# An LSH attention and expert kernel on one core: joint value means, sign words and sums on GpSimd, a new order of the work

## The chip, the cores and the metric

The kernel runs on one core of a Trainium2 chip. The core has a matrix engine (TensorE, "PE" in the rows; its weight loads are "PEld"), a vector engine (VectorE, "DVE"), a scalar engine (ScalarE, "ACT"), a general engine (GpSimd, "POOL"), and a queue engine (SyncE, "SP") that here only issues transfers. Each engine takes its own instructions strictly in the order in which they stand. The metric is the device time of one execution in microseconds (us); the number to forecast is a median over repeated runs. Three runs of the kernel before took 1003.26, 1003.40 and 1003.53 us.

## The reference

Inputs are q, k, v of 4 batches x 8 heads x 768 positions x 64, a 64x6 projection, and the two matrices of a feed-forward layer.

```
q_bucket = sum over 6 bits of 2^bit * (q @ proj > 0)          # k_bucket likewise
mask     = q_bucket[:, None] == k_bucket[None, :]
scores   = where(mask, q @ k.T / 8, -1e9)
attn     = exp(scores - max);  attn /= sum(attn) + 1e-9
x        = attn @ v, heads side by side                       # 3072 x 512
out      = (s * relu(x @ w_in)^2 + b) @ w_out                 # 512 -> 2048 -> 512
```

## The kernel before

**Staging.** There are 32 visits, one for each batch and head, and each has three chunks of 256 queries: 96 slots. A slot computes scores in three PSUM banks (L595 or L597), takes their maximum on VectorE (L603), turns it with small TensorE transposes (L614, L618), adds a row with mask and maximum (L635 or L637), takes exponentials on ScalarE (L642), and multiplies by the values (L665, or L667 and L668) into PSUM bank 3. ScalarE empties that bank (L698, L700); two heads are normalised together on VectorE and GpSimd (L707 to L712) and written to DRAM as `xd`. The first nine visits (`NPL = 9`: batch 0 and one head of batch 1) multiply in whole fp32, where one product shows as two records in the trace; later visits split each operand into a high and a low part and use a faster format.

**The feed-forward layer.** `moe` (L746 and L763) runs chunk by chunk as soon as the eight heads of a batch are done (`GATE = 23`). Its products carry the lowest priority, so TensorE takes them wherever attention leaves room. The weights come as raw 64-bit words and are rebuilt in `decode`, 32 tiles of 128x512: ScalarE makes a shifted value and the scaled low word (L374, L375), VectorE takes the sign bit (L376) and joins it to the shifted word (L377), GpSimd adds the low word (L378), ScalarE rounds to the high part (L380) and GpSimd subtracts it (L386). Two tiles `osb` take turns. All decoding lies in the first 210 us, beside batch 0.

**The mean of the values.** Because of the 1e-9 in the denominator each head adds a constant times the sum of its values (`vmn`, a bias of L700). `prep_values` makes that sum two visits ahead. In the first nine visits TensorE adds six 128x64 value tiles with six one-column products (`sums`, L543). In the 23 later ones VectorE adds the six tiles (L556) and TensorE makes one one-column product (L558). Both write PSUM bank 4, which the small transposes of the scores use as well; the values of later visits arrive in one tile, `vn`.

**The order.** A planner (`Plan`) collects all steps with a cost, inputs, outputs and a priority, and lays them out with a model of five engines. To a step's priority it adds a number from the table `NUDGE`, by the step's place in the source and the part of the program. What comes out is a fixed instruction order for each engine.

Of the kernel before, what the change touches and what calls it, by code (L numbers as in the profile page):

```python
# [15 lines left out]
ALU = mybir.AluOpType  # L16
# [156 lines left out]
def lsh_attention_moe(ctx: ExitStack, tc, q, k, v, proj, w_in, w_out, s, b, out):  # L173
# [43 lines left out]
    def dve(n, fn, r, w, pr, ns=None):  # L217
        plan.add(DVE, ((n + 64) / 960.0 if ns is None else ns), fn, r, w, pr)
# [7 lines left out]
    def mmc(n, c):  # L226
        return c * (n / 2400.0 + 0.0013) if c % 4 == 0 else c * (n * 0.000436 + 0.0088)
# [124 lines left out]
    def decode(u, pr):  # L352
# [23 lines left out]
        dve(256, lambda: nc.vector.tensor_scalar(raw()[:, :, 1], gi, -2**31, None, ALU.bitwise_and), [gk], rk, pr, 0.6)  # L376
        dve(512, lambda: nc.vector.scalar_tensor_tensor(gi, gi, 3, raw()[:, :, 1], ALU.logical_shift_left, ALU.bitwise_or), rk, [gk], pr, 0.92)  # L377
# [8 lines left out]
        pool(512, lambda: nc.gpsimd.tensor_tensor(wt[key][:, 1], g, f32(wt[key][:, 0]), ALU.subtract), [gk, key + (0,)], [key + (1,)], pr)  # L386
# [135 lines left out]
    def mean(bb, h, pr):  # L522

        n = bb % 2 * H + h
        act(1, lambda: nc.scalar.activation(vmn[:, n:n + 1], bank[0:D, 4, 0:1], AF.Copy, scale=EPS / (S + EPS)), [("b", 4, "m")], [("vm", n)], pr)
        plan.hold(None)

    def prep_values(w, pr):
        bb, h = visits[w]["bb"], visits[w]["h"]
        x = visits[w]["x"]  # L530
        vk = [("vs", x, 0), ("vs", x, 1)]
        vd = v[bb, h].rearrange("(p t) d -> p t d", t=NT)
        if w < NPL:
            if x not in SETS:
                def new():
                    EV[x] = wk.tile([P, NT, 2, D], F32, tag=f"vs{x}", name=f"vs{w}")
                plan.add(None, 0.0, new, [], vk, pr)
                pool(1, lambda: nc.gpsimd.memset(EV[x][:, :, 1], 1.0), [], vk[1:2], pr, 0.5)
            plan.add(SP, 0.7, lambda: nc.sync.dma_start(EV[x][:, :, 0], vd), [], vk[0:1], pr, 0.9)

            def sums():
                for t in range(NT):
                    nc.tensor.matmul(bank[0:D, 4, 0:1], EV[x][:, t, 0], ones, start=(t == 0), stop=(t == NT - 1))  # L543
            plan.hold(4)
            pe(0.5, sums, vk, [("b", 4, "m")], pr)
            mean(bb, h, pr)
            return

        def new():
            VS[x] = wk.tile([P, NT, 2, D], F32R, tag=f"vs{x}", name=f"vs{w}")  # L550
        plan.add(None, 0.0, new, [], vk, pr)
        to = vn
        plan.add(SP, 0.7, lambda: nc.sync.dma_start(to, vd), [], ["vn"], pr, 0.9)
        act(NT * D, lambda: nc.scalar.copy(VS[x][:, :, 0, :], to), ["vn"], vk[0:1], pr)
        pool(NT * D, lambda: nc.gpsimd.tensor_tensor(VS[x][:, :, 1, :], to, f32(VS[x][:, :, 0, :]), ALU.subtract), ["vn", vk[0]], vk[1:2], pr)
        dve(NT * D, lambda: nc.vector.tensor_reduce(pj[:, 0:D], to.rearrange("p t d -> p d t"), AX.X, ALU.add), ["vn"], ["vp"], pr, 0.84)  # L556
        plan.hold(4)
        pe(0.25, lambda: nc.tensor.matmul(bank[0:D, 4, 0:1], pj[:, 0:D], ones, start=True, stop=True), ["vp"], [("b", 4, "m")], pr)  # L558
        mean(bb, h, pr)
# [397 lines left out]
```

## Time and profile before

| what | value |
|---|---|
| median of three runs | 1003.4 us |
| the profiled execution's own time | 1000.88 us |
| its span, first to last instruction | 999.1 us |
| TensorE busy | 979.9 us, 98% |
| VectorE, ScalarE, GpSimd busy | 677.5, 670.8, 640.5 us |
| mean granted TensorE clock | 0.998 of full speed |

The span is what the trace shows; 1.8 us of the profiled execution lie around it. The profiled execution was 2.5 us shorter than the median run. Busy time of TensorE counts a matmul from start to its modelled end, and matmuls overlap, so the distance from one start to the next tells more than a duration.

### The profile page before, as it was taken

What the parts mean: (1) busy time and instruction counts of PE and PEld (TensorE: products, weight loads), DVE (VectorE), ACT (ScalarE), POOL (GpSimd) and SP (SyncE); (2) the same over time, 40 slices, a digit from 0 to 9 for tenths busy, and PEclk for the clock granted to TensorE, in tenths of its full rate; (3) what the DMA queues carried; (4) which work ended last, traced back from release to release, by engine and by line L of the source; (5) the groups of instructions that cost most, each with busy time, mean ns of one, the idle gap of its engine ahead of it and who ended that gap; (6) DMA issues with size and microseconds to landing.
All of it is one profiled execution on the core that took longest, in us unless ns stands there. A gap on an engine that the chain in (4) does not pass through costs nothing.

```text
span 999.1 us, 18150 instructions
## 1 busy us (share of the span) xinstructions
PE 979.9 (98%) x6528; PEld 883.6 (88%) x6528; DVE 677.5 (68%) x1030; ACT 670.8 (67%) x1312; POOL 640.5 (64%) x584
## 2 busy tenths in 40 slices
PE   8989989999999999999999999999999999999998
PEld 6877868889999999999999999999999999999997
DVE  6777888778778877878778877878778766200000
ACT  4677777767767777777767777777777777523232
POOL 1677776758677677768677677778677677522222
PEclk9999999999999999999999999999999999999999
DMA  7575664533423423433423432433423310201000
GB/s 195 148 192 162 182 169 129 152 76 82 129 53 79 122 69 63 131 71 81 120 63 79 104 84 61 136 71 81 120 60 80 97 47 1 96 1 64 32 22 21
DMA packets 131954, 93.06 MB, mean 93 GB/s; under 512 B 101145, under 2 KB 104601, under 8 KB 131865
## 3 DMA queue, kind: packets, MB, share of 16 engines
q1 hardware_dynamic: 126664, 74.87, 29.9%
q10 hardware_dynamic: 5200, 17.05, 5.7%
q8 instruction: 51, 0.84, 0.3%
q14 instruction: 39, 0.31, 0.1%
HBM read 48.24 MB, written 18.87 MB: 67 GB/s over the span
## 4 chain that ended last, share of the span: by engine, by line
PE 91%; DVE 2%; POOL 2%; DMA 2%; issue 1%; ACT 1%; DVEq 0%; ACTq 0%; SPq 0%; POOLq 0%
PE bank L746 28%; PE bank L763 27%; PE bank L597 6%; PE bank L637 6%; PE bank L667 5%; PE bank L668 5%; PE bank L665 4%; PE bank L595 2%; PE bank L695 2%; DMA xd<-xsb 1%; PE bank L618 1%; PE bank L506 1%; PE bank L508 1%; PE bank L507 1%; POOL w L386 1%
## 5 line engine op out<-in xcount | busy, mean ns | idle before, releaser
L661 POOL TENSOR_TENSOR hl<-et,hl 128x512 fp32r<-128x512 f32 x207 | 267.3, 1320 | 138.5 <-ACT hl L660 86.0
L746 PE MATMUL bank<-xc,w 128*128 128x256 f32 x2304 | 338.5, 284 | 0.0
L746 PEld LDWEIGHTS bank<-xc,w 128*128 128x128 f32 x2304 | 305.4, 190 | 5.9
L763 PE MATMUL bank<-w,ghb 128*128 128x512 f32 x768 | 252.4, 396 | 0.0
L754 POOL TENSOR_TENSOR glb<-rb,ghb 128x512 fp32r<-128x512 f32 x96 | 124.1, 1292 | 99.8 <-ACT ghb L753 93.7
L603 DVE TENSOR_REDUCE mx<-bank 128x256 f32<-128x1536 f32 x96 | 168.0, 1750 | 6.9 <-PE bank L597 3.2
L763 PE MATMUL bank<-w,glb 128*128 128x512 f32 x384 | 152.3, 398 | 0.0
L642 ACT ACTIVATE et<-bank 128x512 f32<-128x512 f32 x234 | 128.6, 626 | 32.5 <-PE bank L637 23.4
L763 PEld LDWEIGHTS bank<-w,ghb 128*128 128x128 f32 x768 | 135.2, 189 | 16.6 <-issue 0.2
L687 DVE TENSOR_REDUCE zb<-et 128x256 f32<-128x1536 f32 x69 | 120.8, 1751 | 40.9 <-ACT et L642 40.2
L660 ACT CAST hl<-et 128x512 fp32r<-128x512 f32 x207 | 125.2, 672 | 0.3
L751 ACT ACTIVATE rb<-bank 128x512 f32<-128x512 f32 x96 | 56.8, 592 | 98.7 <-PE bank L746 98.4
L597 PE MATMUL bank<-aq,ks 84*128 84x256 f32 x504 | 109.6, 301 | 2.3 <-DMA aq<-nat 1.4
L700 ACT ACTIVATE xpb<-bank,vmn 64x256 f32<-64x256 f32 x96 | 45.0, 468 | 97.4 <-PE bank L668 64.1
L667 PE MATMUL bank<-hl,vs 128*128 128x256 f32 x414 | 107.9, 283 | 0.0
L668 PE MATMUL bank<-hl,vs 128*128 128x256 f32 x414 | 107.3, 281 | 0.0
L597 PEld LDWEIGHTS bank<-aq,ks 84*128 84x128 f32 x504 | 81.0, 190 | 9.1 <-ACT xpb L700 1.8
L667 PEld LDWEIGHTS bank<-hl,vs 128*128 128x128 f32 x414 | 77.9, 188 | 8.9
L668 PEld LDWEIGHTS bank<-hl,vs 128*128 128x128 f32 x414 | 78.0, 188 | 8.0
L763 PEld LDWEIGHTS bank<-w,glb 128*128 128x128 f32 x384 | 72.2, 188 | 11.5 <-issue 0.2
L637 PE MATMUL bank<-bq,ks 128*128 128x256 f32 x504 | 76.9, 287 | 0.0
L771 DVE SCALAR_TENSOR_TENSOR osb<-bank,misc,bcs 128x512 f32<-128x512 f32 x22 | 16.2, 747 | 88.9 <-PE bank L763 88.8
(126 smaller groups left out, 1545.2 us busy)
## 6 DMA issues: line engine op xcount, KB each, us to landing
xd<-xsb SPq DMA_DIRECT2D x48, 256.0 KB
xc<-xd SPq DMA_DIRECT2D x48, 256.0 KB
raw<-in_moe_w_in_dram ACTq DMA_DIRECT2D x16, 512.0 KB
raw<-in_moe_w_out_dram ACTq DMA_DIRECT2D x16, 512.0 KB
out_dram<-osb SPq DMA_DIRECT2D x22, 256.0 KB
ks<-aq SPq DMA_DIRECT2D x28, 192.0 KB
ks<-bq SPq DMA_DIRECT2D x28, 192.0 KB
bq<-aq SPq DMA_DIRECT2D x28, 192.0 KB
```

Source lines behind the costliest of these rows:

```text
L597: nc.tensor.matmul(o, ks[0:HR + NR, 0, kt], aq[0:HR + NR, cs], start=m == 0, stop=m == 1, skip_group_check=True)
L603: dve(S * TPC, lambda: nc.vector.tensor_reduce(t, sc, AX.XY, ALU.max), [("b", b) for b in pb], [tk], pr, 1.75)
L637: nc.tensor.matmul(o, ks[:, 1, kt], bq[:, cs], start=False, stop=m == 1, skip_group_check=True)
L642: act(512, lambda p=p, z=z: nc.scalar.activation(et(z) if plain(i) else pairs(z), bank[:, pb[p]] if plain(i) else bank[:, pb[p]].rearrange ...
L660: act(512, lambda z=z, y=y: nc.scalar.copy(HL[2 * y].rearrange("p (m n) -> p m n", n=CH), pairs(z)), [("e", z)], [("hl", 2 * y)], pr, 0.05)
L661: pool(512, lambda z=z, y=y: nc.gpsimd.tensor_tensor(HL[2 * y + 1].rearrange("p (m n) -> p m n", n=CH), pairs(z), f32(HL[2 * y]).rearrange ...
L667: nc.tensor.matmul(av, VS[x][:, kt], HL[2 * y][:, ms], start=(kt == 0), stop=False)
L668: nc.tensor.matmul(av, VS[x][:, kt], HL[2 * y + 1][:, ms], start=False, stop=(kt == NT - 1))
L687: dve(S * TPC, lambda: nc.vector.tensor_reduce(ZB, es, AX.XY, ALU.add), [("e", z) for z in range(NE)], ["zb"], pr, 1.75)
L746: nc.tensor.matmul(hp, wt[("wi", n, cc)][:, m % 2, fs], xc[:, m // 2, :], start=(cc == 0 and m == 0), stop=(cc == NC_ - 1 and m == 2))
L754: pool(2 * CH, lambda r=r, gh=gh, gl=gl: nc.gpsimd.tensor_tensor(gl, r, f32(gh), ALU.subtract), [rk, hk], [lk], MP)
L763: nc.tensor.matmul(bank[:, 6 + t, :], (gh, gh, gl)[n][:, ts], wt[("wo", f)][:, n % 2], start=(f == 0 and n == 0), stop=(f == NF - 1 and n ...
```

## The change

Three things are edited. For odd and even heads of one batch the two value sums stand side by side in `pj`, and one product with 128 columns of weights instead of 64 gives both means; for it the odd head's values are loaded into `vn` one more time. For visits 2 to 8 GpSimd adds the six value tiles in three instructions (128x192, 128x64, 128x64), and TensorE makes one product instead of six. In `decode` the sign word is made by GpSimd with a comparison and a multiplication. The planner's costs are adjusted, and the table `NUDGE` has new numbers throughout (80 rows before, 84 after).

```
-        return c * (n / 2400.0 + 0.0013) if c % 4 == 0 else c * (n * 0.000436 + 0.0088)
+        return c * (n / 2400.0 + 0.0013) if c % 4 == 0 else c * {256: 0.1215, 384: 0.175, 512: 0.2345}[n]
...
-        dve(256, lambda: nc.vector.tensor_scalar(raw()[:, :, 1], gi, -2**31, None, ALU.bitwise_and), [gk], rk, pr, 0.6)
-        dve(512, lambda: nc.vector.scalar_tensor_tensor(gi, gi, 3, raw()[:, :, 1], ...), rk, [gk], pr, 0.92)
+        pool(512, lambda: nc.gpsimd.tensor_scalar(raw()[:, :, 1], g, 0.0, -2.0**31, ALU.is_lt, ALU.mult), [gk], rk, pr, 0.65)
+        dve(512, lambda: nc.vector.scalar_tensor_tensor(gi, gi, 3, raw()[:, :, 1], ...), rk, [gk], pr, 0.8)
...
+            if w > 1:
+                s1, s2 = vn[:, 0:3], vn[:, 3]
+                pool(3 * D, lambda: nc.gpsimd.tensor_tensor(s1, EV[x][:, 0:3, 0], EV[x][:, 3:6, 0], ALU.add), vk[0:1], ["vn"], pr, 0.56)
+                pool(D, lambda: nc.gpsimd.tensor_tensor(s2, vn[:, 0], vn[:, 1], ALU.add), [], ["vn"], pr, 0.27)
+                pool(D, lambda: nc.gpsimd.tensor_tensor(s2, vn[:, 3], vn[:, 2], ALU.add), [], ["vn"], pr, 0.27)
+                plan.hold(4)
+                pe(0.3, lambda: nc.tensor.matmul(bank[0:D, 4, 0:1], s2, ones, start=True, stop=True), ["vn"], [("b", 4, "m")], pr)
+                mean(bb, h, pr)
...
+        if h % 2 and w > NPL:
+            return
+        heads = (h,) if h % 2 else (h, h + 1)
+        for j, h_ in enumerate(heads):
+            if j:
+                fetch(to, tk, v[bb, h_].rearrange("(p t) d -> p t d", t=NT))
+            sums(j, to, tk)
+        rows = len(heads) * D
         plan.hold(4)
-        pe(0.25, lambda: nc.tensor.matmul(bank[0:D, 4, 0:1], pj[:, 0:D], ones, start=True, stop=True), ["vp"], [("b", 4, "m")], pr)
-        mean(bb, h, pr)
+        pe(0.3, lambda: nc.tensor.matmul(bank[0:rows, 4, 0:1], pj[:, 0:rows], ones, start=True, stop=True), ["vp"], [("b", 4, "m")], pr)
+        for j, h_ in enumerate(heads):
+            mean(bb, h_, pr, j)
...
-    0: {0: -25.2, 1: 58.1, 2: 23.3, 3: 60, 4: -47.5},
+    0: {0: -6.4, 1: -4.1, 2: -23.8, 3: -11.2, 4: 11},
```

Line numbers move: in the changed kernel the sign word is still L376 and the join L377, but scores' transposes are L640 and L644 (were L614, L618), the row that is added is L651 on VectorE (was L625) and L661 or L663 on TensorE (were L635, L637), attention times values in fp32 is L691 (was L665), the means are L546, L553 and L582 (were L543 and L558).

In the first decodes, GpSimd's order before, with the add L378 and the subtraction L386 (`raw` and `w` with their buffer numbers):

```order
L378 TENSOR_TENSOR osb<-osb,raw_209 128x512
L386 TENSOR_TENSOR w_365<-osb,w_365 128x512
L386 TENSOR_TENSOR w_377<-osb,w_377 128x512
L378 TENSOR_TENSOR osb<-osb,raw_210 128x512
L386 TENSOR_TENSOR w_433<-osb,w_433 128x512
L378 TENSOR_TENSOR osb<-osb,raw_211 128x512
```

And there in the changed kernel, with the sign word L376 and, ahead of it, the three adds of a head's values:

```order
L542 TENSOR_TENSOR vn<-vs_213 128x192
L543 TENSOR_TENSOR vn<-vn 128x64
L544 TENSOR_TENSOR vn<-vn 128x64
L376 TENSOR_SCALAR raw_207<-osb 128x512
L376 TENSOR_SCALAR raw_209<-osb 128x512
L378 TENSOR_TENSOR osb<-osb,raw_207 128x512
L386 TENSOR_TENSOR w_368<-osb,w_368 128x512
L378 TENSOR_TENSOR osb<-osb,raw_209 128x512
L376 TENSOR_SCALAR raw_210<-osb 128x512
L386 TENSOR_TENSOR w_387<-osb,w_387 128x512
L378 TENSOR_TENSOR osb<-osb,raw_210 128x512
```

The sign word of a tile stands ahead of the subtraction of the tile before it.

VectorE at the same place before, where `mx`, `nmt` and `zhl` belong to the scores:

```order
L616 TENSOR_REDUCE nmt<-bank 128x2
L376 TENSOR_SCALAR raw_211<-osb 128x512
L625 SCALAR_TENSOR_TENSOR zhl<-bank,ident 8x256
L377 SCALAR_TENSOR_TENSOR osb<-osb,raw_211 128x512
L603 TENSOR_REDUCE mx<-bank 128x256
```

And in the changed kernel:

```order
L377 SCALAR_TENSOR_TENSOR osb<-osb,raw_211 128x512
L629 TENSOR_REDUCE mx<-bank 128x256
L642 TENSOR_REDUCE nmt<-bank 128x2
L377 SCALAR_TENSOR_TENSOR osb<-osb,raw_212 128x512
L651 SCALAR_TENSOR_TENSOR zhl<-bank,ident 8x256
L629 TENSOR_REDUCE mx<-bank 128x256
```

The join L377 now stands without its sign word, directly ahead of the row `zhl` (L651) that TensorE needs.

TensorE before, at the mean of visit 3 in batch 0:

```order
L637 MATMUL bank<-bq_70,ks_72 128x256 x2
L543 MATMUL bank<-misc,vs_213 64x1 x6
L637 MATMUL bank<-bq_70,ks_72 128x256 x4
L665 MATMUL bank<-ex_84,vs_208 128x256
L496 MATMUL bank<-eqa,pj 128x384
```

And the mean of one of batch 0's visits in the changed kernel:

```order
L623 MATMUL bank<-aq_68,ks_72 128x256 x2
L644 MATMUL bank<-ident,nmt 8x128
L546 MATMUL bank<-misc,vn 64x1
L663 MATMUL bank<-bq_70,ks_72 128x256 x6
L458 MATMUL bank<-ident,nat_66 128x128 x3
```

Six one-column products on the value tile are one on `vn`, and it stands between the transpose of the maximum (L644) and the products that need it (L663).

## Rows read from the trace of the kernel before

**Rows 1.** The page's first part: busy us (share of the span) and instructions.

```profile
PE 979.9 (98%) x6528; PEld 883.6 (88%) x6528; DVE 677.5 (68%) x1030; ACT 670.8 (67%) x1312; POOL 640.5 (64%) x584
```

**Rows 2.** Windows: stretch, length, busy us (instructions) by engine, clock, DMA share, GB/s.

```profile
0.00:200.00 200.00, 184.37 (x1073) 153.55 (x1074) 155.32 (x257) 141.37 (x280) 128.45 (x116) 0.99 0.63 166
200.00:850.00 650.00, 650.00 (x4534) 598.56 (x4533) 511.87 (x756) 478.02 (x948) 472.28 (x436) 1.00 0.33 83
850.00:1000.00 150.00, 145.51 (x925) 131.53 (x923) 10.27 (x18) 51.40 (x87) 39.73 (x34) 0.99 0.11 39
...
100.00:150.00 50.00, 45.62 (x267) 36.96 (x266) 42.01 (x63) 37.97 (x76) 37.73 (x33) 1.00 0.65 176
```

**Rows 3.** Waits of TensorE: who for whom, us in total, times, longest.

```profile
PE bank L665 <- ACT xpb L700: 4.2, 5, 2.1
PE bank L597 <- DMA aq<-nat: 1.4, 1, 1.4
...
PE bank L472 <- DVE bq L625: 1.1, 1, 1.1
PE bank L472 <- DVE zhl L625: 1.1, 2, 0.6
...
PE bank L614 <- DVE mx L603: 0.3, 1, 0.3
```

**Rows 4.** Timeline from 63.6 us: start, us, instruction, idle time before and its releaser.

```profile
64.85 0.40 ACT L711 CAST xsb<-xpb 128x256 fp32r<-128x256 f32 x1 [1.99 <-DMA xd<-xsb]
...
65.68 0.47 ACT L700 ACTIVATE xpb<-bank,vmn 64x256 f32<-64x256 f32 x1
...
66.29 0.65 PE L665 MATMUL bank<-et,vs 128*128 128x256 f32 x1 [2.06 <-ACT xpb L700]
```

**Rows 5.** Timeline of TensorE from 10.5 us, at one of the six-product sums.

```profile
11.69 0.55 PE L458 MATMUL bank<-ident,nat 128*128 128x128 f32 x3
12.16 0.86 PE L543 MATMUL bank<-misc,vs 128*64 128x1 f32 x12
12.95 0.59 PE L496 MATMUL bank<-eqb,pj 128*128 128x384 f32 x1
```

**Rows 6.** Timeline of TensorE from 700.2 us, at one single-head mean.

```profile
701.48 0.90 PE L637 MATMUL bank<-bq,ks 128*128 128x256 f32 x6
702.32 0.28 PE L558 MATMUL bank<-misc,pj 128*64 128x1 f32 x2
702.52 0.50 PE L746 MATMUL bank<-xc,w 128*128 128x256 f32 x2
702.86 0.40 PE L597 MATMUL bank<-aq,ks 84*128 84x256 f32 x2
```

**Rows 7.** Groups by line and form: count | busy us, mean ns | idle before.

```profile
L763 PEld LDWEIGHTS bank<-w,ghb 128*128 128x128 f32 x768 | 135.2, 189 | 16.6 <-issue 0.2
...
L712 POOL TENSOR_TENSOR xsb<-xpb,xsb 128x256 fp32r<-128x256 f32 x48 | 37.7, 785 | 6.9 <-ACT xsb L711 6.3 <-PE bank L695 0.5
...
L376 DVE TENSOR_SCALAR raw<-osb 128x512 int32<-128x512 int32 x32 | 23.1, 720 | 0.2
...
L385 POOL TENSOR_TENSOR bcs<-bcs,osb 128x512 f32<-128x512 f32 x15 | 19.8, 1322 | 1.0
...
L558 PEld LDWEIGHTS bank<-misc,pj 128*64 128x64 f32 x46 | 4.4, 134 | 3.3 <-issue 0.4
...
L383 POOL COPY bcs<-osb 128x512 f32<-128x512 f32 x1 | 0.6, 609 | 0.1
```

**Rows 8.** Line 376 by itself: duration in ns, least/median/most, first and last start.

```profile
L376 DVE TENSOR_SCALAR raw<-osb x32: 373/478/1848, 21.5 to 202.4; 128x512 int32<-128x512 int32 x32
```

**Rows 9.** Waits of GpSimd and ScalarE in the decode chain.

```profile
POOL osb L378 <- DVE osb L377: 35.1, 13, 18.8
...
ACT osb L374 <- POOL w L386: 8.5, 13, 2.1
...
ACT w L380 <- POOL osb L378: 5.4, 6, 2.0
```

More of the change, by code (lines that the diff above doesn't have):

```diff
@@ L375, in decode @@
         act(512, lambda: nc.scalar.activation(raw()[:, :, 0], raw()[:, :, 0].bitcast(U32), AF.Copy, scale=float(2.0**-29)), rk, rk, pr, 0.06)
-        dve(256, lambda: nc.vector.tensor_scalar(raw()[:, :, 1], gi, -2**31, None, ALU.bitwise_and), [gk], rk, pr, 0.6)
-        dve(512, lambda: nc.vector.scalar_tensor_tensor(gi, gi, 3, raw()[:, :, 1], ALU.logical_shift_left, ALU.bitwise_or), rk, [gk], pr, 0.92)
+        pool(512, lambda: nc.gpsimd.tensor_scalar(raw()[:, :, 1], g, 0.0, -2.0**31, ALU.is_lt, ALU.mult), [gk], rk, pr, 0.65)
+        dve(512, lambda: nc.vector.scalar_tensor_tensor(gi, gi, 3, raw()[:, :, 1], ALU.logical_shift_left, ALU.bitwise_or), rk, [gk], pr, 0.8)
         pool(512, lambda: nc.gpsimd.tensor_tensor(gi, gi, raw()[:, :, 0], ALU.add), rk, [gk], pr)
@@ L385, in decode @@
                 pool(512, lambda: nc.gpsimd.tensor_tensor(bcs, bcs, g, ALU.add), [gk], ["bcs"], pr + 5)
-        pool(512, lambda: nc.gpsimd.tensor_tensor(wt[key][:, 1], g, f32(wt[key][:, 0]), ALU.subtract), [gk, key + (0,)], [key + (1,)], pr)
+        pool(512, lambda: nc.gpsimd.tensor_tensor(wt[key][:, 1], g, f32(wt[key][:, 0]), ALU.subtract), [gk, key + (0,)], [key + (1,)], pr, 1.43)
     def bias(pr):
@@ L520, in prep, with mean @@
         return [lambda i, pr, f=f, g=g: f(g, i, pr) for f, n in ((both, 2), (hash_, 2)) * exact + ((split, 2), (hash_, 2)) * (not exact) for g in range(n)]
-    def mean(bb, h, pr):
+    def mean(bb, h, pr, j=0):
         n = bb % 2 * H + h
-        act(1, lambda: nc.scalar.activation(vmn[:, n:n + 1], bank[0:D, 4, 0:1], AF.Copy, scale=EPS / (S + EPS)), [("b", 4, "m")], [("vm", n)], pr)
-        plan.hold(None)
+        act(1, lambda: nc.scalar.activation(vmn[:, n:n + 1], bank[j * D:(j + 1) * D, 4, 0:1], AF.Copy, scale=EPS / (S + EPS)), [("b", 4, "m")], [("vm", n)], pr)
     def prep_values(w, pr):
@@ L539, in prep_values @@
             plan.add(SP, 0.7, lambda: nc.sync.dma_start(EV[x][:, :, 0], vd), [], vk[0:1], pr, 0.9)
+            if w > 1:
[6 more added lines that the diff above has]
+                mean(bb, h, pr)
+                plan.hold(None)
+                return
             def sums():
@@ L544, in prep_values @@
             plan.hold(4)
-            pe(0.5, sums, vk, [("b", 4, "m")], pr)
+            pe(0.75, sums, vk, [("b", 4, "m")], pr)
             mean(bb, h, pr)
+            plan.hold(None)
             return
@@ L551, in prep_values, with fetch, sums @@
         plan.add(None, 0.0, new, [], vk, pr)
[L552 to L556, printed above, removed]
+        to, tk = vn, "vn"
+        def fetch(to, tk, vd):
+            plan.add(SP, 0.7, lambda: nc.sync.dma_start(to, vd), [], [tk], pr, 0.9)
+        def sums(j, to, tk):
+            dve(NT * D, lambda: nc.vector.tensor_reduce(pj[:, j * D:(j + 1) * D], to.rearrange("p t d -> p d t"), AX.X, ALU.add), [tk], ["vp"], pr, 0.84)
+        fetch(to, tk, vd)
+        act(NT * D, lambda: nc.scalar.copy(VS[x][:, :, 0, :], to), [tk], vk[0:1], pr)
+        pool(NT * D, lambda: nc.gpsimd.tensor_tensor(VS[x][:, :, 1, :], to, f32(VS[x][:, :, 0, :]), ALU.subtract), [tk, vk[0]], vk[1:2], pr)
+        if h % 2 and w > NPL:
+            return
+        heads = (h,) if h % 2 else (h, h + 1)
[4 more added lines that the diff above has]
+        rows = len(heads) * D
         plan.hold(4)
-        pe(0.25, lambda: nc.tensor.matmul(bank[0:D, 4, 0:1], pj[:, 0:D], ones, start=True, stop=True), ["vp"], [("b", 4, "m")], pr)
-        mean(bb, h, pr)
+        pe(0.3, lambda: nc.tensor.matmul(bank[0:rows, 4, 0:1], pj[:, 0:rows], ones, start=True, stop=True), ["vp"], [("b", 4, "m")], pr)
+        for j, h_ in enumerate(heads):
+            mean(bb, h_, pr, j)
+        plan.hold(None)
     def plain(i):
```

162 rows, old and new, of the table NUDGE are left out of this document.

## The prediction

> **What bounds the kernel now.** I read the busy times first: TensorE is busy for 979.9 of 999.1 us, the next engine for 677.5 [rows 1]. Then I cut the span into stretches. From 200 to 850 us TensorE is busy in all 650 us, at full clock; from 850 on feed-forward products alone run, and the 4.5 us without a matmul are the last output's way out. What idle time there is otherwise lies in the first 200 us: 200 less 184.4 makes 15.6 us [rows 2]. There batch 0 runs with the decoding beside it, and no feed-forward product is yet there to fill a hole.
>
> So the kernel is two things. After 200 us a matmul less is time less, and a delay on another engine costs nothing while its cover lasts. Before 200 us the time is TensorE's work plus what it waits for. The waits by name show what these are: 15 kinds that sum to the 15.6 us within rounding, from 4.2 us for ScalarE's emptying of bank 3 down to 0.3 us, with VectorE's part in the scores in several of them [rows 3]. The longest is worth a look: TensorE stood 2.06 us for the emptying at 65.68, and that instruction was late since ScalarE had stood 1.99 us, two instructions ahead, for the transfer that frees `xsb` [rows 4]. An engine that takes its work in order passes a wait on to whatever stands behind it; this is where the change can do harm.
>
> **One product for two heads' means.** A single-head product shows as two records. The six products ahead of one take 0.90 us and two of the same width 0.40, so one more adds 0.125, and the six give way at 701.48 + 0.75 = 702.23. The next product starts at 702.52, and the one after its pair 0.34 us later where two should take 0.25. A mean thus costs 0.29 + 0.09 = 0.38 us of TensorE [rows 6]. Before there are 23, afterwards 12: one alone and eleven joint ones.
>
> A joint product loads 128 columns of weights where the single one loads 64, twice. In the rows the wider load lasts 189 ns, the narrower 134 [rows 7]: 2 x 0.055 = 0.11 us more. Eleven pairs go from 22 x 0.38 = 8.4 to 11 x 0.49 = 5.4 us: 3.0 us less. All of it lies where TensorE never idles, so I count it in full. The bounds: 11 x 0.38 = 4.2 us if the wider load costs nothing, 0 if a joint product costs as much as two.
>
> The Trainium skill weighs against this term. Its page "TensorE: Matmul & The Clock Gate" (section LDWEIGHTS) says that a weight load takes its columns divided by 1.2 per nanosecond, whatever their height: 107 ns for 128 columns, 53 for 64. The difference, 54 ns, is that of the two rows, so the trace agrees. If a mean were nothing but its loads, joining would save nothing, by that rule; the 0.38 us of [rows 6] is far more than two loads of 53 ns, so most of a mean is the break in the stream, and that is paid once for two heads.
>
> What it adds: VectorE's reductions stay 23, ScalarE's bias copies stay one for each head. The odd heads' values are fetched again, eleven more transfers of 192 KB, and the second fetch of a pair must wait until `vn` has been read for the first; behind it in SP's queue stand the loads of q and k and the copies that scores need. Behind a late joint product on TensorE stands everything. In the trace no mean is among the 15 waits, and the one wait for such a copy cost 1.4 us [rows 3]. Bounds: 0 to 11 x 1.4 = 15.4 us. I take 0, nearest to 23 means without a wait.
>
> **Sums on GpSimd.** A six-product sum starts at 12.16 and the next product at 12.95: 0.79 us [rows 5]. One product's two records take 0.20 us to the next start [rows 6]. Seven visits go from 0.79 to 0.20: 4.1 us of TensorE, all in the first 200 us. There a shorter stream partly turns into a longer wait, so the bounds are 0 and 4.1; I take 2.0. GpSimd pays: its 128x256 operations last 785 ns [rows 7], so three smaller ones lie between 0.98 us by width (0.59 + 2 x 0.20) and 2.36 us at the full price; I take 1.1, near the first, 7.7 us in all (6.9 to 16.5). TensorE's product now waits for that sum, with score products queued behind it.
>
> **Sign words.** VectorE loses 32 x 0.72 = 23.1 us [rows 7], nearly all in the first 200 us. The 0.72 is a stretched number: the shortest of them took 0.373 us, the median 0.478, the longest 1.848 [rows 8]. GpSimd's price for a comparison with a multiplication isn't in the trace. The nearest rows are its one-input copy of the same shape, 609 ns, and its two-input add, 1322 ns [rows 7]. The new operation has one input, so I take 0.61: 32 x 0.61 = 19.5 us, at most 42.3.
>
> The Trainium skill speaks against it: "GPSIMD Engine Reference" (section 4.1, Engine selection) says that elementwise work belongs on VectorE, GpSimd being about twice as slow with two inputs and roughly as fast with one. Its section 3.1 (Elementwise) gives 769 ns for 512 elements in a tight loop, an estimate of 32 x 0.769 = 24.6 us here, against 19.5 by the copy's row. The page's section 1 (Specifications) speaks for the move: GpSimd shares its SBUF interfaces with VectorE, with contention in VectorE's two-port modes. The spread of [rows 8], from 0.373 to 1.848 us for one operation of one shape, agrees with that.
>
> GpSimd is busy for 128.5 us of the first 200, VectorE for 155.3 [rows 2]. With 19.5 and 7.7 more GpSimd has 155.7, with the upper bounds 187; VectorE has 132.2. From 100 to 150 us GpSimd has 37.7 of 50 [rows 2]; a quarter of the added 27.2 brings it to 44.5, 89%. That is tight but fits, for GpSimd stood 35.1 us waiting for VectorE's join (18.8 of them before the first decode, so some 16 in the loop) [rows 9], and the sign words go into such holes. And what VectorE loses brings its part of the scores forward. Against it: the join now waits for GpSimd, and in the changed order it stands directly ahead of the row `zhl` that TensorE's score products need. ScalarE's wait for the subtraction, 8.5 us, and for the add, 5.4 [rows 9], can grow as well, and they hold the exponentials and the emptying of bank 3 behind them. I count this part and the new order together, since both act on the 15.6 us alone. From 8 us gained to 12 lost is open; as VectorE, the busier of the two, gets relief, I take 2.0 us gained.
>
> After 200 us a new order can gain nothing, since nothing is idle there, and lose only if feed-forward products run out early. In the order before, 855 products of the feed-forward layer stand behind the last one of attention, in the changed order 860, so they don't, and I put 0.
>
> **The sum.** 3.0 + 2.0 + 2.0 = 7.0 us less: the profiled execution goes from 1000.88 to 993.9, and the median, which lay 2.5 us over it, from 1003.4 to 996.4.
>
> **Rivals.**
> 1. The first stage was held by VectorE. Then relief takes half of the 15.6 us, 7.8, and sums and pairs count in full: 1003.4 - 7.8 - 4.1 - 3.0 = 988.5. For it: VectorE has the longest busy time beside TensorE there [rows 2] and stands behind many of the waits. Against it: the largest waits are for ScalarE and a transfer [rows 3, 4], which get no relief.
> 2. GpSimd becomes the bound of the first stage: the place is VectorE's join, held by a sign word that stands behind GpSimd's other work, and with it `zhl` and TensorE's score products. It decides when a sign word comes later than VectorE is free for it. One uncovered sign word of 0.61 us for each of 32 tiles is 19.5 us on VectorE; if two thirds reach TensorE, 13.0 us are lost, the sums' 4.1 go into the waits, and the pairs' 3.0 remain: 1003.4 + 13.0 - 3.0 = 1013.4. With a third, 6.5 us, it is 1006.9, and that I take as its likely value. For it: 89% load and a longer path between two engines. Against it: the sign word stands a whole subtraction ahead of the add that follows it, and GpSimd's waits show room.
> 3. Nothing measurable: the saved sums turn into waits, and the joint means wait for their second fetch by 0.27 us each, 11 x 0.27 = 3.0, which eats the pairs' gain: 1003.4. For it: the two mechanisms above exist; against it, 23 means of before never waited.
>
> **How the numbers follow.** The forecast, 996.4, has a chance of 0.54 and its own range from 991 to 1001. Rival 1 has 0.15, rival 2 0.18, rival 3 0.13. A difference of under 0.2%, 2 us, can't be told from none in this kernel. Forecast and rival 1 but for 0.01 are faster by more: 0.68. Rival 3 and a little of the neighbours make 0.14 within, rival 2 0.18 slower. The range that leaves two in ten out cuts the far side of rival 2 and the lower half of rival 1: 988.5 to 1007.
>
> **What would show it.** 11 joint means and one single one with no wait of TensorE ahead of them, and a joint one costing about 0.49 us from the product ahead to the stream behind. TensorE's idle time in the first 200 us at 12 to 15 us; at over 20, rival 2 is right, and the waits will name VectorE's row `zhl` or ScalarE behind GpSimd. GpSimd's sign word near 0.61 us; near 1.3, the first stage is GpSimd's. VectorE's busy time falls by about 23 us, GpSimd's rises by 27. The forecast is wrong if TensorE idles between 200 and 850 us at all.

## The result, and the profile after

The changed kernel took 1015.4 us (median of four runs, 1014.5 to 1015.6) beside 1003.5 us of the kernel before on the same chip (1003.3 to 1004.1): a ratio of 1.0116, with a 95% interval from 1.0099 to 1.0134. It is slower by about 12 us, where 996.4 was forecast and a range that ended at 1007.

First the page's busy times, which answer to [rows 1], and the share of each engine in the chain that ended last.

```profile
PE 979.2 (97%) x6436; PEld 880.1 (87%) x6436; DVE 674.6 (67%) x998; ACT 677.7 (67%) x1312; POOL 711.2 (70%) x637
...
PE 79%; POOL 13%; issue 2%; DVE 2%; DMA 2%; ACT 1%; DVEq 0%; POOLq 0%; SPq 0%; ACTq 0%
```

Two entries are odd, and GpSimd's share of the chain, 13%, was 2% before. GpSimd has 70.7 us more, where 27 were forecast. VectorE has only 2.9 less, where 23 were. The windows, which answer to [rows 2], tell where: stretch, length, busy us and instructions of PE, PEld, DVE, ACT and POOL, granted clock, share and rate of the transfers.

```profile
50.00:100.00 50.00, 39.77 (x213) 31.33 (x212) 36.19 (x48) 34.02 (x68) 47.71 (x41) 0.98 0.56 153
100.00:150.00 50.00, 43.49 (x226) 35.16 (x225) 32.04 (x48) 32.99 (x65) 47.74 (x41) 0.95 0.56 151
150.00:200.00 50.00, 43.16 (x218) 35.01 (x217) 38.92 (x52) 34.10 (x67) 48.44 (x40) 0.93 0.55 152
200.00:850.00 650.00, 649.05 (x4524) 597.83 (x4525) 515.06 (x761) 487.89 (x958) 484.87 (x443) 1.00 0.36 90
...
0.00:200.00 200.00, 170.09 (x890) 137.55 (x890) 139.85 (x205) 128.56 (x250) 175.49 (x153) 0.97 0.58 154
```

From 50 to 200 us GpSimd is busy for 47.7 to 48.4 of every 50, 95 to 97%: in this kernel it is nearly full there. TensorE has 170.1 of the first 200, so it idles for 29.9 us where it idled for 15.6, and gets through 890 matmuls instead of 1073. Of these 183, 70 are records that the sums no longer need (seven visits, 12 records before and 2 now); the others are work left for later. After 200 us it is as full as before, as forecast; what the first stage didn't do is done at the end.

The groups by form say what GpSimd does there (count | busy us, mean ns of one | idle time before them and what ended it).

```profile
L376 POOL TENSOR_SCALAR raw<-osb 128x512 int32<-128x512 f32 x32 | 62.7, 1961 | 4.7 <-ACT osb L374 4.7
L386 POOL TENSOR_TENSOR w<-osb,w 128x512 fp32r<-128x512 f32 x32 | 44.8, 1399 | 1.9 <-ACT w L380 1.6 <-DMA nat<-in_q_dram 0.2
...
L377 DVE SCALAR_TENSOR_TENSOR osb<-osb,raw 128x512 int32<-128x512 int32 x32 | 41.3, 1291 | 25.1 <-POOL raw L376 24.1 <-DMA xd<-xsb 0.9
...
L542 POOL TENSOR_TENSOR vn<-vs 128x192 f32<-128x192 f32 x5 | 3.9, 779 | 6.1 <-DMA vs<-in_v_dram 6.0
```

A sign word takes 1961 ns on GpSimd; 610 were taken, and 1322 named as the most. The 32 of them are 62.7 us. VectorE's join (line 377), which reads that word, had a mean of 791 ns before and has 1291 now: 16 of the 23 us that VectorE gave away it spends again on slower joins. Now the waits in the decode chain, which answer to [rows 9] (who for whom, us in total, times, longest).

```profile
DVE osb L377 <- POOL raw L376: 24.1, 21, 2.8
ACT osb L374 <- POOL w L386: 21.0, 18, 2.5
ACT w L380 <- POOL osb L378: 16.6, 15, 2.6
```

VectorE waits 24.1 us for sign words, a wait that did not exist. ScalarE waits 21.0 us for the subtraction, where it was 8.5, and 16.6 for the add, where it was 5.4. How that reaches TensorE shows in a timeline of all engines from 160 us (start, duration, instruction, in brackets the idle time before it and its releaser).

```profile
162.88 1.94 POOL L376 TENSOR_SCALAR raw<-osb 128x512 int32<-128x512 f32 x1
...
164.79 1.28 POOL L378 TENSOR_TENSOR osb<-osb,raw 128x512 int32<-128x512 int32 x1
164.86 1.76 DVE L377 SCALAR_TENSOR_TENSOR osb<-osb,raw 128x512 int32<-128x512 int32 x1 [2.80 <-POOL raw L376]
166.10 0.62 ACT L380 CAST w<-osb 128x512 fp32r<-128x512 f32 x1 [1.81 <-POOL osb L378]
...
166.62 1.56 ACT L668 ACTIVATE ex<-bank 128x512 f32<-128x512 f32 x3
...
167.27 1.22 PE L621 MATMUL bank<-eqb,ekb 128*128 128x256 f32 x2 [3.72 <-ACT ex L668]
```

The window of the four microseconds behind it:

```profile
168.00:172.00 4.00, 4.00 (x12) 3.17 (x11) 2.16 (x5) 2.54 (x5) 3.92 (x5) 0.50 0.02 5
```

GpSimd's sign word ends at 164.82 and VectorE, which stood 2.80 us for it, starts its join. GpSimd's add runs beside that join, on another tile. ScalarE stands 1.81 us for the add with its copy, and behind that copy stand the three exponentials that empty the score banks. TensorE needs those banks for its next scores and stands for 3.72 us. In the window behind that hole its granted clock is 0.50, the lower of its two levels (1.2 GHz). Eight score products show it, earlier in the kernel and then behind the hole, where they last twice as long:

```profile
30.82 1.89 PE L621 MATMUL bank<-eqb,ekb 128*128 128x256 f32 x8
...
167.27 3.78 PE L621 MATMUL bank<-eqb,ekb 128*128 128x256 f32 x8 [3.72 <-ACT ex L668]
```

Of TensorE's waits these answer to [rows 3]:

```profile
PE bank L691 <- ACT ex L668: 4.5, 4, 1.8
PE bank L621 <- ACT ex L668: 3.7, 1, 3.7
PE bank L640 <- DVE mx L629: 2.4, 2, 1.6
...
PE bank L661 <- DVE zhl L651: 1.1, 2, 0.6
...
PE bank L546 <- POOL vn L544: 0.2, 1, 0.2
```

The first two are ScalarE's exponentials, late behind its copies; before, the longest wait was 2.1 us [rows 3]. The 24 kinds of wait in this view come to 30.5 us over the whole span: 19.0 of them end with VectorE's instructions and 11.3 with ScalarE's, where before it was 6.4 and 7.3. So ScalarE makes the longest single hole, but most of the growth comes by way of VectorE, many small waits for its part of the scores.

The three windows of 50 us give the clock's share: 0.02, 0.05 and 0.07 below full speed, times 50, make 7.0 us; before, 0.01 of 200 makes 2.0 [rows 2]. Both are estimates from two decimals.

### The profile page after: what moved, and what is told of

Same layout as the page of the kernel before. It is cut to its first block, busy times and chain, and to the rows that moved or that the text cites. A ratio compares the mean times of both kernels' runs of the same rounds, so it can differ in the third digit from the quotient of the medians.

```text
span 1013.8 us, 18000 instructions
## 1 busy us (share of the span) xinstructions
PE 979.2 (97%) x6436; PEld 880.1 (87%) x6436; DVE 674.6 (67%) x998; ACT 677.7 (67%) x1312; POOL 711.2 (70%) x637
## 4 chain that ended last, share of the span: by engine, by line
PE 79%; POOL 13%; issue 2%; DVE 2%; DMA 2%; ACT 1%; DVEq 0%; POOLq 0%; SPq 0%; ACTq 0%
PE bank L772 26%; PE bank L789 26%; PE bank L623 5%; PE bank L663 5%; PE bank L694 5%; PE bank L693 5%; POOL raw L376 5%; POOL osb L378 3%; POOL w L386 2%; PE bank L721 2%; POOL bcs L385 1%; PE bank L691 1%; DVE osb L377 1%; PE bank L506 1%; PE bank L508 1%
## 5 line engine op out<-in xcount | busy, mean ns | idle before, releaser
L772 PE MATMUL bank<-xc,w 128*128 128x256 f32 x2304 | 333.8, 283 | 0.0
L789 PE MATMUL bank<-w,ghb 128*128 128x512 f32 x768 | 256.0, 397 | 0.0
L668 ACT ACTIVATE et<-bank 128x512 f32<-128x512 f32 x234 | 131.6, 626 | 23.8 <-PE bank L663 16.5
L686 ACT CAST hl<-et 128x512 fp32r<-128x512 f32 x207 | 130.1, 659 | 0.8
L693 PE MATMUL bank<-hl,vs 128*128 128x256 f32 x414 | 110.3, 287 | 0.0
L694 PE MATMUL bank<-hl,vs 128*128 128x256 f32 x414 | 108.5, 282 | 0.0
L623 PEld LDWEIGHTS bank<-aq,ks 84*128 84x128 f32 x504 | 80.9, 190 | 10.6 <-ACT et L668 3.8
L663 PE MATMUL bank<-bq,ks 128*128 128x256 f32 x504 | 77.2, 288 | 1.0 <-DVE bq L651 1.0
L663 PEld LDWEIGHTS bank<-bq,ks 128*128 128x128 f32 x504 | 67.9, 189 | 6.0 <-DVE bq L651 2.2
```

Of the source, the lines that this page charges most:

```text
L623: nc.tensor.matmul(o, ks[0:HR + NR, 0, kt], aq[0:HR + NR, cs], start=m == 0, stop=m == 1, skip_group_check=True)
L663: nc.tensor.matmul(o, ks[:, 1, kt], bq[:, cs], start=False, stop=m == 1, skip_group_check=True)
L668: act(512, lambda p=p, z=z: nc.scalar.activation(et(z) if plain(i) else pairs(z), bank[:, pb[p]] if plain(i) else bank[:, pb[p]].rearrange ...
L686: act(512, lambda z=z, y=y: nc.scalar.copy(HL[2 * y].rearrange("p (m n) -> p m n", n=CH), pairs(z)), [("e", z)], [("hl", 2 * y)], pr, 0.05)
L693: nc.tensor.matmul(av, VS[x][:, kt], HL[2 * y][:, ms], start=(kt == 0), stop=False)
L694: nc.tensor.matmul(av, VS[x][:, kt], HL[2 * y + 1][:, ms], start=False, stop=(kt == NT - 1))
```

## The experiments

Three kinds of kernel: some let the order of the work be planned anew, some hold the instructions of every engine in the order that they had and change one thing, and two time GpSimd's instructions by themselves. All ratios are to the kernel before, with 95% intervals.

**The sign word, with the order planned anew (three runs).** The first takes the sign word back to VectorE, the second puts it alone into the kernel before, the third tells the planner a price near the true one.

```
e1: - pool(512, lambda: nc.gpsimd.tensor_scalar(raw()[:, :, 1], g, 0.0, -2.0**31, ALU.is_lt, ALU.mult), ..., 0.65)
    + dve(256, lambda: nc.vector.tensor_scalar(raw()[:, :, 1], gi, -2**31, None, ALU.bitwise_and), ..., 0.6)
    (and the join's cost 0.8 -> 0.92)
e2: the reverse of it, in the kernel before
e3: - ... ALU.is_lt, ALU.mult), [gk], rk, pr, 0.65)
    + ... ALU.is_lt, ALU.mult), [gk], rk, pr, 1.96)
```

> The changed kernel with the sign word made by VectorE again, as before; joint means, GpSimd's sums, planner costs and the new table stay. Theory: the whole loss comes from the sign word, which takes 1.96 us on GpSimd and fills it in the first 235 us. Then GpSimd falls back to about 136 us of the first 200, TensorE's idle time in the first 200 us to 12 to 18 us, and the time is what was forecast without the sign word, 996 to 999 us. Rival A, the new order itself is bad: 1008 us or more. Rival B, the sums on GpSimd do a share of the harm: between, 1000 to 1008 us.

> The kernel before with the sign word alone on GpSimd; its own table of priorities, no joint means, no sums on GpSimd. Theory: GpSimd gets 32 x 1.96 = 63 us more and is full for the first 225 us; loss of 15 us or more, 1015 to 1030 us. Rival A (the new order did it): within 4 us of 1003.4. Rival B: half of the loss, 1008 to 1012 us.

> The changed kernel, but the planner is told that the sign word costs 1.96 us on GpSimd in place of 0.65; the program does the same work in an order planned with that. Theory (the load itself binds): GpSimd still has about 175 us in the first 200, so it stays at 1008 us or over. Rival C (the work fits, only the order was laid out for a wrong price, so that VectorE and ScalarE stand behind it): 1002 us or less.

Measured: e1 1014.2 us, ratio 1.0111 [1.0094, 1.0129]; e2 1024.5, 1.0212 [1.0193, 1.0232]; e3 1033.7, 1.0306 [1.0285, 1.0328]. Read alone, e1 says that the sign word costs nothing, and the theory would have fallen. But e3 changes no instruction, only a number that the planner reads, and costs 18 us more than the kernel after. The table of numbers that sets the order was searched for one set of costs; with another set it gives an order nobody searched. So e1 and e2 changed two things at once, and by themselves they decide nothing. From here on the orders are held.

**The sign word in the order of after.** Each engine's other instructions stay where they are. In e5 the word is planned as GpSimd's and issued on VectorE; in e6 GpSimd makes a cheaper word of another operation pair.

```
e5: + pool(512, lambda: nc.vector.tensor_scalar(raw()[:, :, 1], gi, -2**31, None, ALU.bitwise_and), ..., 0.65)
e6: + pool(512, lambda: nc.gpsimd.tensor_scalar(raw()[:, :, 1], g, 0.0, 0.0, ALU.add, ALU.mult), ..., 0.65)
```

> The changed kernel with the sign word made by VectorE, while the planner still plans it for GpSimd: the orders on TensorE, ScalarE and SP stay word for word those of the changed kernel, and VectorE and GpSimd differ in these 32 instructions alone. In the first experiment every order was planned anew as well, by a table searched for another plan. Theory: the 1.96 us on GpSimd make the loss; held so, the time falls to 996 to 1003 us, GpSimd's busy time in the first 200 us to 115 to 130, TensorE's granted clock there back to 0.99. Rival A (the new order is bad in itself): 1008 us or more.

> The changed kernel, all five orders held, with the compare-and-multiply on GpSimd replaced by add-and-multiply of the same shape and output, which took 0.62 us; the sign is left out (the word is zero), nothing else. This is the price that the forecast had assumed (0.61). Theory: the price of the sign word alone was mis-sized, so the time comes to 993 to 1000 us. Rival A (order): 1008 us or more. Rival B (any sign word on GpSimd harms, by the wait of VectorE for it): 1003 to 1008 us.

Measured: e5 996.2 us, 0.9934 [0.9912, 0.9956]; e6 991.6, 0.9894 [0.9876, 0.9912]. Both are faster than the kernel before, so the sign word on GpSimd alone turns the rest of the change from a gain into a loss: 18 us against e5 and 22 against e6 by the ratios. The first 200 us of e5, then of e6:

```profile
0.00:200.00 200.00, 181.29 (x1003) 151.81 (x1004) 156.80 (x263) 140.92 (x277) 134.13 (x134) 0.98 0.63 169
```

```profile
0.00:200.00 200.00, 184.59 (x1019) 154.82 (x1020) 146.93 (x234) 142.93 (x282) 155.66 (x167) 0.98 0.62 170
```

The group of e6's sign word, and the join's wait for it:

```profile
L376 POOL TENSOR_SCALAR raw<-osb 128x512 int32<-128x512 f32 x32 | 22.1, 693 | 5.7 <-ACT osb L374 5.7
```

```profile
DVE osb L377 <- POOL raw L376: 1.3, 3, 0.7
```

With 0.69 us a word GpSimd has 155.7 us of the first 200, the very number of the forecast, VectorE's join waits 1.3 us instead of 24.1, and TensorE idles for 15.4 in the first 200 us. So it isn't the place of the work that hurts, nor the longer path between two engines, but the duration of this operation. At 991.6 us e6 is a little better than its expectation (993 to 1000); e5 meets its own in time, though GpSimd has 134.1 us where 115 to 130 were expected. e5 leaves nothing out and beats both kernels; it is the version to keep.

**The sign word in the order of before.** The same two words on GpSimd, with nothing else of the change.

```
e7: - dve(256, lambda: nc.vector.tensor_scalar(raw()[:, :, 1], gi, -2**31, None, ALU.bitwise_and), ..., 0.6)
    + dve(256, lambda: nc.gpsimd.tensor_scalar(raw()[:, :, 1], g, 0.0, -2.0**31, ALU.is_lt, ALU.mult), ..., 0.6)
e8: + dve(256, lambda: nc.gpsimd.tensor_scalar(raw()[:, :, 1], g, 0.0, 0.0, ALU.add, ALU.mult), ..., 0.6)
```

> The kernel before with the sign word on GpSimd as in the change (1.92 to 1.96 us), all orders of before held but for these 32 instructions. Theory: GpSimd goes from 128 to about 180 us of the first 200 and the time rises by 12 to 25 us, 1015 to 1028. Rival A: within 4 us of 1003.5.

> As the last one, with add-and-multiply (0.62 us) in the place of compare-and-multiply; the sign is left out, nothing else. It tells what a sign word on GpSimd at the price of the forecast would have done by itself. Theory: 1000 to 1005 us, no loss. Rival B (the wait of VectorE for GpSimd harms at any price): 1008 us or more.

Measured: e7 1029.5 us, 1.0272 [1.0250, 1.0294]; e8 1004.0, 1.0020 [1.0006, 1.0035]. The group of e7's sign word and the join's wait:

```profile
L376 POOL TENSOR_SCALAR raw<-osb 128x512 int32<-128x512 f32 x32 | 62.7, 1958 | 14.2 <-ACT osb L374 14.2
```

```profile
DVE osb L377 <- POOL raw L376: 35.4, 20, 3.2
```

Its first 200 us:

```profile
0.00:200.00 200.00, 167.59 (x928) 133.55 (x928) 128.49 (x196) 125.78 (x243) 159.21 (x130) 0.98 0.55 148
```

e7 lies just over its expected range, and one part of the expectation missed: GpSimd has 159.2 us of the first 200 and not 180. That is hardly more than the 155.7 of e6, which loses nothing. So GpSimd need not be full for the loss. The slow word lengthens the chain of each tile, and the decoding lasts longer: the last sign word starts at 231.0 us in e7 and at 204.7 in e8. In e8 the join waits 11.1 us for its words, and the time hardly moves.

By the ratios the loss from cheap to dear is 25 us here and 22 in the order of after, for 41 us more of GpSimd's sign words in both (62.7 less 21.3 and 22.1): about 0.6 us of time for each us. The order of after does not make the sign word cheap; it makes a quick word worth something (e6 beats e5 by 4.6 us, where e8 is 0.2% slower than before).

**Which operations are slow on GpSimd.** Two kernels put single instructions of 128x512 ahead of the work, each form twice, on data that nothing reads.

```
e4: is_lt+mult to int, strided (the sign word's form) | to int, dense | to f32, dense
    add+mult | mult alone | is_lt alone | copy to int | mult alone to int
e9: mult+min to int, strided | mult+min | max+min | max+mult | mult+add | is_lt+add | subtract+mult
```

> The kernel before with sixteen extra GpSimd instructions ahead of the decoding, eight forms twice on 128x512, whose results are overwritten; only their durations are of interest, not the time. Forms: compare and multiply into every second integer word; the same into dense integers; the same into dense floats; add and multiply; multiply alone; compare alone; copy to integers; multiply to integers. If the two operations make the price, add and multiply takes about 1.9 us and one operation about 0.6 to 1.0; if the conversion to integers does, the float forms take 0.6 to 0.7 and the integer copy 1.9; if the stride does, the dense forms take 0.6 to 0.7; if the comparison does, compare alone stands out.

> The kernel before with fourteen extra GpSimd instructions ahead of the decoding, seven forms twice on 128x512; only their durations count. The first set showed add-and-multiply at 0.62 us, compare-and-multiply at 1.92, a lone multiply or compare at 1.49 to 1.50, a copy to integers at 0.61. Forms now: multiply and minimum into every second integer word, the same into dense floats, maximum and minimum, maximum and multiply, multiply and add, compare and add, subtract and multiply. If only pairs of add, subtract and multiply are quick, forms with minimum, maximum or a comparison take 1.5 us or more; if the comparison alone is slow, minimum and maximum take 0.62 as well.

Second pass of e4, in the order of the list; all forms but the copy read alike, so the line number tells them apart:

```profile
17.28 1.97 POOL L328 TENSOR_SCALAR osb<-rb 128x512 int32<-128x512 f32 x1
...
21.34 1.92 POOL L330 TENSOR_SCALAR osb<-rb 128x512 f32<-128x512 f32 x1
23.34 0.62 POOL L331 TENSOR_SCALAR osb<-rb 128x512 f32<-128x512 f32 x1
24.04 1.50 POOL L332 TENSOR_SCALAR osb<-rb 128x512 f32<-128x512 f32 x1
25.62 1.49 POOL L333 TENSOR_SCALAR osb<-rb 128x512 f32<-128x512 f32 x1
27.18 0.61 POOL L334 CAST osb<-rb 128x512 int32<-128x512 f32 x1
```

Of e9, max+mult and then mult+add:

```profile
24.17 1.92 POOL L331 TENSOR_SCALAR osb<-rb 128x512 f32<-128x512 f32 x1
26.17 0.62 POOL L332 TENSOR_SCALAR osb<-rb 128x512 f32<-128x512 f32 x1
```

Neither the stride (1.97 against 1.92) nor the conversion (1.92 both ways) makes the sign word slow. Of the pairs that were run, the two of an add and a multiplication took 0.62; every one with a comparison, a minimum, a maximum or a subtraction took 1.92 to 1.97; a single operation took 1.49 to 1.50, so one operation costs more than add and multiplication together. The hope for a quick pair that makes a sign word, mult+min, fell with its 1.97.

**The same price by another pair.** e10 holds the order of after and makes the word with mult+min, the smaller of 2^100 times the value and 0; the word it makes isn't the sign, so its time alone is read.

```
e10: + pool(512, lambda: nc.gpsimd.tensor_scalar(raw()[:, :, 1], g, 2.0**100, 0.0, ALU.mult, ALU.min), ..., 0.65)
```

> [...] If that form is quick (0.62 to 0.70 us), the time is that of the cheap word, 989 to 994 us, with the sign in it; if it takes 1.5 us, GpSimd gets about 27 us more than with the cheap word and the time is 1000 to 1010.

Measured: 1024.5 us, 1.0210 [1.0197, 1.0224], 9 us over the kernel after and beyond both ranges that were expected.

```profile
L376 POOL TENSOR_SCALAR raw<-osb 128x512 int32<-128x512 f32 x32 | 63.6, 1988 | 7.3 <-ACT osb L374 4.7
...
L377 DVE SCALAR_TENSOR_TENSOR osb<-osb,raw 128x512 int32<-128x512 int32 x32 | 22.2, 695 | 36.4 <-POOL raw L376 36.4
```

A price of 1.99 again makes the kernel slower than before, as the theory has it, but not by the same amount. VectorE's joins wait longer here (36.4 against 24.1 us) and then run quickly (695 against 1291 ns), so slow joins are not what the time hangs on. The sign words add one us to GpSimd, but with the adds and subtractions of the decoding it is 154.5 us against 149.7, and the last sign word starts at 234.3 us instead of 225.8. The windows show where the 9 us come to light on TensorE:

```profile
0.00:200.00 200.00, 166.22 (x854) 134.46 (x854) 118.02 (x196) 121.37 (x237) 175.73 (x146) 0.95 0.56 151
200.00:850.00 650.00, 646.84 (x4498) 595.17 (x4499) 513.13 (x763) 488.21 (x959) 486.80 (x444) 1.00 0.36 91
```

It idles 3.9 us more than in after in the first 200 us (33.8 less 29.9) and 2.2 more up to 850, and by windows of 50 us the clock takes some 3.0 more (10.0 less 7.0). Why the same order with a word of nearly the same price waits longer stays open.

**The joint means: what a wider weight load costs.** The kernel before with its 23 single means, each loading 128 columns of weights in place of 64; the upper 64 results are not read.

```
e11: - nc.tensor.matmul(bank[0:D, 4, 0:1], pj[:, 0:D], ones, start=True, stop=True)
     + nc.tensor.matmul(bank[0:P, 4, 0:1], pj[:, 0:P], ones, start=True, stop=True)
```

> The kernel before with its 23 single-head means over 128 columns of weights in place of 64 (the upper 64 results are not read); orders held. In the trace a single 64-column mean costs TensorE 0.40 us of the stream and a joint 128-column one 0.23. Theory: the narrow shape itself breaks the stream, so 23 wide ones save 23 x 0.17 = 3.9 us: 997 to 1001 where before is 1001.6 to 1003.7 (ratio 0.996). Rival, the working of the forecast: a wider load costs 0.11 us more, so 2.5 us are lost (ratio 1.0025).

Measured: 999.8 us, 0.9963 [0.9951, 0.9975]. Twice the weights, and 3.7 us faster: 0.16 us for each mean. The wider product was quicker, so the 0.11 us that the forecast charged it for its load do not show.

**The sums on GpSimd.** e5 once more, with six products on TensorE for each sum and without GpSimd's three adds.

```
e12: e5, and  - pool(...tensor_tensor(s1, ...)), pool(...tensor_tensor(s2, ...)) twice
              + the six products over EV[x][:, t, 0] in place of the one over s2
```

> The changed kernel with the sign word on VectorE as in the fifth run, and in visits 2 to 8 the value sums again as six products on TensorE, GpSimd's three adds gone; orders held but for these. Against the fifth run (ratio 0.9934 to before) it tells what the sums on GpSimd are worth. The forecast had 2.0 us of 4.1: ratio 0.995 to 0.996. If all 4.1 us count, 0.9975; if they lay in waits, 0.993 to 0.994; if the adds on GpSimd harm, below 0.993.

Measured: 998.3 us, 0.9943 [0.9926, 0.9960], beside e5's 0.9934 [0.9912, 0.9956]. The sums are worth 0.9 us by the difference, and the intervals overlap, so this is not told from nothing.

## Why the prediction was wrong

**The step that failed** is the price of the sign word. "The nearest rows are its one-input copy of the same shape, 609 ns, and its two-input add, 1322 ns", and from them 0.61 was taken and 42.3 us named as the most for 32 words. The copy has the same shape and one input, and in e4 a copy that converts to integers as well takes 0.61 us; the sign word's pair of operations takes 1.92 there, and 1.97 into every second word. The measured 62.7 us lie outside both ends that the two neighbours of [rows 7] gave, so the range was no bound. e6 turns the reading round: at 0.69 us a word the same kernel gains 10.6 us by its ratio, where 7.0 were forecast. With 62.7 in the forecast's own sum, GpSimd's load in the first 200 us would have come to 128.5 + 62.7 + 7.7 = 198.9: no room at all, which is rival 2's case. The Trainium skill's figure that the prediction weighed ("GPSIMD Engine Reference", section 3.1, Elementwise: 769 ns for 512 elements) was short too, by 1961 against 769 ns. Its advice in section 4.1 (Engine selection), to leave elementwise work to VectorE, agrees with e5 against the kernel after, 0.9934 against 1.0116. It does not hold for every operation: e6, with a quick pair on GpSimd, has 0.9894.

**Rival 2** had the right mechanism and the chance of 0.18, and the range, which ended at 1007, cut off its 1013.4. It named VectorE's join, held by a sign word behind GpSimd's other work, and the point from which it decides. Its 1013.4 is near by way of a wrong price: at 0.61 us it did not come about (e6), at 1.96 it did. So its nearness to 1015.4 is luck in part. About 0.6 of GpSimd's added time reached the end; the rival's two thirds were of another sum, 19.5 us of waits on VectorE. The way to TensorE was hardly the row `zhl` (1.4 us of its waits). It was ScalarE, whose copies stand behind the add and ahead of the exponentials, as in the timeline at 164 us, and more of it VectorE's other work on the scores, 17.6 us of waits for `mx`, `nmt`, `bq`, `eka` and the like. [Rows 4] had shown this passing on of a wait.

**The joint means** were right in sign and too small: 3.0 us forecast, bounds 0 to 4.2. The trace of after gives a joint product's price, here between feed-forward products at 684 us.

```profile
683.73 0.40 PE L789 MATMUL bank<-w,ghb 128*128 128x512 f32 x1
683.97 0.28 PE L693 MATMUL bank<-hl,vs 128*128 128x256 f32 x1
...
684.43 0.40 PE L789 MATMUL bank<-w,ghb 128*128 128x512 f32 x1
684.66 0.28 PE L582 MATMUL bank<-misc,pj 128*128 128x1 f32 x2
684.80 0.48 PE L789 MATMUL bank<-w,glb 128*128 128x512 f32 x1
685.12 0.28 PE L693 MATMUL bank<-hl,vs 128*128 128x256 f32 x1
```

The product at 684.43 gives way after 0.23 us, as the one at 683.73 does after 0.24. The joint mean takes 0.14 to the next start, and the product behind it 0.32 where 0.24 is usual: 0.22 us in all. Counted in this way over the whole trace, the typical single mean of before costs 0.40 us and the typical joint one 0.23; the wide single means of e11 cost 0.23 as well. So 23 x 0.40 = 9.2 became 11 x 0.23 + 0.40 = 2.9: 6.3 us saved. The forecast had the 0.40 nearly right (0.38) and added 0.11 for the wider load, from the durations of two load rows [rows 7]. Loads run beside products; their duration is no price. The rule of the Trainium skill ("TensorE: Matmul & The Clock Gate", section LDWEIGHTS: columns divided by 1.2 per ns) gives the difference of those rows, 54 against 55 ns, though not the 189 and 134 themselves; but the time went the other way, in e11 by 3.7 us. That the narrow product is the dear one no row of before had shown, since none of the wide form stood there. The feared waits for the second fetch did not come: line 582 is in none of TensorE's waits, and VectorE's reductions waited 1.6 us in all for fetches of values. That no mean was among the 15 waits of before holds for the 23 means, not for the six-product sums: line 543 is there with 0.5 us.

**The sums** were forecast at 2.0 us, bounds 0 to 4.1; measured 0.9, not told from 0. GpSimd's three adds cost 9.9 us in all where 7.7 were taken.

**The new order** was put together with the sign words at 2.0 us gained. e5 is 6.6 us faster than before by its ratio, and means and sums alone make 6.3 + 0.9 = 7.2; within the noise nothing is left for the order by itself. With a quick word (e6) the kernel is 4.6 us faster than e5.

**After 200 us** the forecast nearly held: 649.05 of 650 us busy. The 0.95 us of idle time are, taken strictly, one of the signs that it had named for being wrong.

**The account.** The two profiled executions lie 14.7 us apart (spans of 1013.8 and 999.1), more than the 11.9 of the medians. TensorE's idle time makes +15.4 (34.6 less 19.2; 14.3 of it in the first 200 us, 1.0 up to 850), its busy time -0.7. Within the busy time the clock is about +5.0 (7.0 less 2.0), the means are -6.3 and the sums, at the forecast's 0.79 and 0.20, -4.1: together -5.4. So 4.7 us of longer work on TensorE are not assigned.

## What to carry to other kernels

Here a price taken from a neighbour of the same shape did not hold for another operation: where the trace has no row of the same engine with the same operations, time that instruction by itself before the sum is made, and take no row of another operation as a bound; GpSimd's dearest row of that shape before, the subtraction of line 386 with 1429 ns, would have been short too. When one part of a change is tested in a planned kernel, hold the order of everything else; a new plan with the same instructions cost 18 us here (e3), about as much as the part that was to be tested. Ask of a small product not how much it loads but how its shape sits in the stream around it.

## What the runs showed of the hardware

- GpSimd on 128x512 elements with one input: add+mult and mult+add 0.62 us, a copy 0.61, a single multiplication or comparison 1.49 to 1.50, and pairs with a comparison, minimum, maximum or subtraction 1.92 to 1.97. The first one in e4 and in e9 took 2.79 and 2.80; in the kernel after, no sign word took more than 2.00, so this is no general price.
- A one-column product with 64 columns of weights, set into a stream of products with 128, costs about 0.40 us; the same with 128 columns costs about 0.23. Widening it without using the result made the kernel 3.7 us faster (0.9963 [0.9951, 0.9975]).
- VectorE's join took 791 ns before, 1291 in after, 819 in e5 and 695 in e10. The Trainium skill ("GPSIMD Engine Reference", section 1, Specifications) says that GpSimd's SBUF interfaces are shared with VectorE. After against e5 agrees with it; but e10 has as much work on GpSimd as after and the quickest joins, so the amount of GpSimd's work does not set the join's duration. What does was not taken apart.
- A hole of 3.72 us on TensorE was followed by a stretch at a granted clock of 0.50, in which eight score products took 3.78 us instead of 1.89.
